# One tile mode at a time: padding PV's last keys, tails as entries of their own, and a new order for the first stretch

## The chip, the cores and the metric

The kernel runs on one core of a Trainium2 chip. The metric is device time in microseconds of one execution. The core's engines are TensorE (PE, with its weight loads PEld), VectorE (DVE), ScalarE (ACT), GpSimd (POOL) and SyncE (SP, which here only issues transfers). Each works through its own instructions in a fixed order and waits on semaphores for the others.

## The reference

Three layers follow each other. First attention with a memory: for 2 batches and 8 heads, 576 positions of 64 numbers,

```python
scores = scale * np.matmul(q, k.transpose(0, 1, 3, 2))
scores = np.where(causal, -1000000000.0, scores)
scores = scores - scores.max(-1, keepdims=True)
a = np.exp(scores)
a /= a.sum(-1, keepdims=True) + 1e-09
local = np.matmul(a, v)
mem_ret = np.einsum('bhsd,bhde->bhse', q_p, M_prev)     # q_p = phi(q)
mem_norm = np.einsum('bhsd,bhd->bhs', q_p, z_prev)[..., None] + 1e-06
return g * (mem_ret / mem_norm) + (1 - g) * local
```

Then, on the 1152 rows of 512 numbers that come out, `(x @ w1) * (x @ w2) @ w3 @ w_out` with weights given as 64-bit floats, and at last four experts, `p[:, e] * (relu(x @ w1[e]) @ w2[e])` summed over e. All of it is in 32-bit floats.

## The kernel before

**Stages.** The first stretch holds attention for all eight pairs of heads, the product W = w3 @ w_out (parts `w`), and the products of batch 0 with w1 and w2 (parts `b`). Then come W's product with batch 0 (`k`, tile `c`), the same for batch 1 (tiles `Zb`, `Rb`, `Qb`), and the four experts (tiles `Z`, `Q`, `R`, `o`).

**A pair of heads.** 576 positions are four blocks of 128 and one of 64. The two heads of a pair lie on partitions 0 to 63 and 64 to 127 of the query and key tiles. For pair p the parts are: `sp0` to `sp3`, scores of query blocks (0, 1), 2, 3 and of the last 64 queries of both heads (`scores`, tile `sc`); `mp*`, a masked reduction on VectorE that also copies the scores out of PSUM (`peaks`, tiles `P` and `mn`); `xp*`, the exponential on ScalarE; `tp0` to `tp6`, transposes of the probabilities in groups of up to four (`trans`, tile `pt`), and `cp*`, their copies to SBUF on ScalarE (tile `pT`); `vp0`, `vp1`, `vp2`, probabilities times V for head 0, head 1 and the last block of both (`pv`, `pv_last`, tile `a`); `np`, the memory product (`mem`, tile `b`); `jp`, `gp`, the divisions on VectorE (`join`, `mem_out`); `jap`, their sum on POOL; `zp`, the transposes of the result (`fin`, tile `x`), with `zhp` and `zlp` copying and splitting it.

**Shapes on TensorE.** Scores of the first four blocks contract over 64 partitions, so a head uses half of the array's rows. `pv` makes 64 output rows at a time: half of its columns. The last two matmuls of `pv_last` (j == NB) contract over 64 keys and make 64 rows: a quarter. The group `t6` transposes 64 columns. `mem` and `fin` end with a tail of two matmuls onto half of the columns. Everything else uses the whole array. 32-bit matmuls leave two records each in the trace, transposes and the bit-split products (`fp32r`) one.

**Weights.** 64-bit weights are rebuilt as floats: two ScalarE operations (`wa`, `oa`, `ba`: lines 129 and 130), two on VectorE (`wd`, `od`, `bd`: lines 136 and 137), then a split in a high and a low part, on POOL for w3, w1, w2 (`wp`, `bp`) and on ScalarE and VectorE for w_out (`oh`, `ol`). One tile of w3 feeds four groups of three matmuls (`wu_0` to `wu_3`), one of w1 or w2 two groups of twelve.

**What sets the order.** The string FIRST, written out by a planner, lists every part and every load (`@...`) of the first stretch; the program records the parts in this order, and each engine keeps it as its own queue. Nothing is reordered later. Tiles come from pools: `psS` has two PSUM buffers for scores, PV, memory and result tiles, `psT` two for transposes, so a part also waits for the reader of what its buffer held before.

Of the kernel before, what the change touches and what calls it, by code (L numbers as in the profile page):

```python
# [20 lines left out]
@o1 s11 c00 wp0 c02 t01 m10 @o2 x03 t04 c01 s12 @w1 c04 m11 x10 t03 m12 v00 @mz c03 x11 t05 @bt v01 c05 x12 t06 t10
s13 c06 c10 e2 v02 m13 @q3 oa0 t14 gates j0 @k3 t13 c14 n0 @V2 x13 od0 t11 t12 s20 g0 c11 @o3 c12 oa1 m20 v10 ja0 c13
x20 t16 v11 f2 oh0 od1 t15 e3 s21 c15 ol0 @w2 c16 oa2 v12 m21 w0_0 oh1 j1 @V3 x21 s22 od2 s23 m22 t20 wa1 @w3 t22 m23
c20 n1 @k4 x22 wd1 @q4 s30 c22 g1 wp1 @w4 x23 t24 oh2 t21 m30 z0 c24 c21 ja1 t23 zh0 v20 c23 zl0 x30 f3 v21 oa3 ol1
t25 ol2 t26 s31 c25 od3 c26 w0_1 hq4 hk4 v22 m31 lq4 @w5 wa2 w0_2 j2 s32 @V4 lk4 x31 n2 oh3 m32 e4 t30 wd2 x32 z1 t32
g2 c30 @w6 wa3 t31 ol3 s33 zh1 zl1 m33 wd3 c31 w0_3 @k5 c32 t34 ja2 y0 @w7 t33 c34 w1_0 c33 v30 @o4 f4 wa4 wp2 v31 x33
@b0 t35 @q5 z2 wd4 c35 @k6 t36 w1_1 zh2 @q6 wa5 w1_2 zl2 w1_3 c36 wd5 e5 n3 y1 wp3 v32 g3 w2_0 @V5 j3 w2_1 wa6 w2_2 f5
w2_3 w3_0 y2 wd6 w3_1 e6 w3_2 wp4 w3_3 s40 y3 wp5 s41 wa7 m40 w4_0 m41 w4_1 x40 ja3 w4_2 w4_3 x41 wd7 w5_0 y4 z3 wp6
oa4 w5_1 w5_2 zh3 w5_3 od4 w6_0 y5 w6_1 zl3 wp7 oh4 @o5 w6_2 ba0 w6_3 s42 ol4 y6 bd0 w7_0 w7_1 m42 oa5 bp0 @b1 w7_2
w7_3 x42 bs0 s43 od5 b0_0 y7 hk5 m43 @o6 oh5 lk5 b0_1 ba1 ol5 @k7 hq5 t40 bd1 x43 t41 n4 c40 lq5 c41 @b2 oa6 t44 g4  # L30
t43 bs1 bp1 c44 s50 @q7 bc00 bc01 t42 m50 v40 c42 c43 od6 x50 b1_0 f6 @b3 oh6 b1_1 ba2 ol6 rm00 e7 bd2 t45 rh00 v41
c45 rl00 ba3 @b4 rm01 bp2 s51 t46 rh01 bs2 m51 c46 v42 rl01 x51 bd3 b2_0 @V6 j4 ba4 bp3 @b5 b2_1 bc20 bs3 s52 bd4 bc21
b3_0 m52 ja4 ba5 @o7 b3_1 x52 bs4 rm10 bp4 rh10 s53 rm11 bd5 rl10 rh11 b4_0 hk6 hq6 rl11 oa7 @b6 b4_1 m53 bp5 x53 bs5
t54 bc40 t50 od7 bc41 c54 b5_0 c50 lq6 oh7 @b7 ba6 b5_1 rm20 bd6 ol7 rh20 t52 t51 c52 n5 rl20 c51 @w8 rm21 bp6 ba7 t53
g5 bs6 v50 rh21 c53 lk6 b6_0 rl21 bd7 b6_1 bc60 f7 wa8 @w9 t55 bp7 v51 bc61 bs7 c55 t56 s60 c56 wd8 b7_0 m60 wa9 wp8
@w10 v52 rm30 x60 b7_1 j5 @V7 rh30 wd9 w8_0 w8_1 rl30 wa10 @w11 w8_2 rm31 wp9 w8_3 rh31 s61 s62 wd10 w9_0 rl31 wa11
@w12 w9_1 m62 wp10 w9_2 y8 w9_3 x62 m61 ja5 s63 yh8 w10_0 m63 x61 w10_1 wd11 hq7 w10_2 hk7 w10_3 yl8 @w13 wa12 t64
wp11 y9 t62 z4 c64 yh9 t60 c62 wd12 n6 c60 x63 yl9 w11_0 @w14 wa13 g6 wp12 w11_1 w11_2 zh4 y10 w11_3 zl4 lq7 yh10
w12_0 w12_1 wd13 w12_2 w12_3 yl10 wa14 @w15 t61 t63 wp13 y11 z5 c61 yh11 v60 c63 wd14 zh5 w13_0 yl11 w13_1 wa15 @b8
zl5 wp14 w13_2 y12 w13_3 yh12 t65 v61 wd15 c65 w14_0 yl12 ba8 @b9 w14_1 wp15 y13 w14_2 yh13 w14_3 yl13 w15_0 bd8 w15_1  # L40
w15_2 y14 lk7 ba9 @b10 w15_3 t66 yh14 bp8 bs8 s70 c66 v62 m70 b8_0 yl14 y15 x70 bd9 s71 ba10 bp9 @b11 m71 b8_1 yh15
bs9 j6 x71 s72 yl15 t70 bd10 bc80 s73 bc81 c70 b9_0 m72 ja6 ba11 @b12 m73 x72 bs10 bp10 b9_1 rm40 rh40 x73 t71 rl40
b10_0 rm41 c71 bd11 rh41 b10_1 rl41 ba12 @b13 bp11 bc100 t74 bs11 bc101 t73 c74 z6 bd12 b11_0 zh6 bp12 @b14 ba13 zl6
b11_1 rm50 bs12 rh50 bd13 t72 b12_0 rl50 c72 @b15 rm51 bp13 c73 rh51 ba14 v70 bs13 rl51 bd14 t75 bc120 v71 c75 ba15
bs14 t76 n7 c76 bd15 b12_1 g7 bs15 v72 bc121 bp14 b13_0 j7 ja7 b13_1 rm60 rh60 rl60 z7 rm61 bp15 rh61 b14_0 zh7 zl7
b14_1 rl61 bc140 b15_0 bc141 b15_1 rm70 rh70 rl70 k00_0 rm71 rh71 k00_1 rl71 k00_2 k00_3 k01_0 kc00 k01_1 k01_2 k01_3
k10_0 kc01 k10_1 k10_2 k10_3 k11_0 kc10 k11_1 k11_2 k11_3 k20_0 kc11 k20_1 k20_2 k20_3 k21_0 kc20 k21_1 k21_2 k21_3
k30_0 kc21 k30_1 k30_2 k30_3 k31_0 kc30 k31_1 k31_2 k31_3 kc31
# [1115 lines left out]
```

## Time and profile before

| what | value |
|---|---|
| three runs | 686.61, 687.25, 687.84 us; median 687.25 |
| the profiled execution: span on the page | 685.4 us |
| its own time outside the span | not given; the median of the runs is 1.85 us above the span |
| busy TensorE, VectorE, ScalarE, POOL | 675.7, 447.5, 382.5, 368.6 us |
| first stretch (attention, w, b) | until 206.78 us, where the product `c` starts |

The page names for each group of instructions its source line, engine, operation and tiles. Times in the timeline are microseconds from the first instruction. A matmul's duration runs past the start of the next one, since they are pipelined: what a matmul costs is the distance from its start to the next start.

### The profile page before, as it was taken

The numbers are of one execution on the slowest core, as the hardware profiler recorded it, in microseconds if no ns is written. First come the engines' busy times: TensorE is split into PE (matmuls) and PEld (weight loads), VectorE is DVE, ScalarE is ACT, GpSimd is POOL, SyncE is SP. The second block draws the span as 40 slices with busy tenths as digits, with TensorE's granted clock in tenths as the row PEclk, the third lists the DMA queues.
The fourth block names the chain that finished last, engine by engine and source line by source line (L and its number), as shares of the span: only waits on it lengthen the run. The fifth ranks groups of instructions, "written<-read, shape, count | busy, mean of one in ns | idle before, by whom it ended". The sixth has DMA issues, their size and how long they took to land.

```text
span 685.4 us, 12814 instructions
## 1 busy us (share of the span) xinstructions
PE 675.7 (99%) x4877; PEld 605.1 (88%) x4877; DVE 447.5 (65%) x839; ACT 382.5 (56%) x808; POOL 368.6 (54%) x366
## 2 busy tenths in 40 slices
...
GB/s 286 176 169 219 71 198 192 174 109 124 185 139 34 90 62 94 55 35 98 62 62 123 77 109 62 112 73 107 79 121 64 62 124 64 122 61 109 154 32 62
DMA packets 43405, 74.53 MB, mean 109 GB/s; under 512 B 14416, under 2 KB 14416, under 8 KB 43344
## 3 DMA queue, kind: packets, MB, share of 16 engines
...
## 4 chain that ended last, share of the span: by engine, by line
PE 88%; DVE 6%; ACT 3%; issue 1%; DMA 1%; SPq 0%; DVEq 0%; ACTq 0%
PE o L990 28%; PE Z L1037 14%; PE c L587 7%; PE Q L1037 7%; PE wacc L473 7%; PE ab L537 5%; PE Zb L853 4%; PE R L1037 3%; PE a L330 2%; PE pt L307 2%; PE Qb L853 2%; PE sc L253 2%; ACT P L274 1%; DVE P L269 1%; PE Rb L853 1%
## 5 line engine op out<-in xcount | busy, mean ns | idle before, releaser
L990 PE MATMUL o<-w,he 128*128 128x512 f32 x864 | 224.8, 393 | 0.0
L104 POOL TENSOR_TENSOR w<-r,w 128x512 fp32r<-128x512 f32 x96 | 130.6, 1361 | 120.3 <-ACT w L728 120.2
L990 PEld LDWEIGHTS o<-w,he 128*128 128x128 f32 x864 | 153.8, 188 | 24.1
L975 ACT ACTIVATE he<-t 128x320 fp32r<-128x320 f32 (+1 forms) x96 | 42.7, 445 | 120.6 <-DVE t L1066 73.3
L976 DVE SCALAR_TENSOR_TENSOR he<-t,he 128x320 fp32r<-128x320 f32 (+1 forms) x96 | 57.4, 598 | 49.1 <-ACT he L975 49.1
L1059 DVE TENSOR_TENSOR t<-u,Q 128x320 f32<-128x320 f32 (+1 forms) x32 | 14.6, 455 | 83.2 <-ACT u L1057 83.2
L107 DVE TENSOR_TENSOR w<-r,w 128x512 fp32r<-128x512 f32 x64 | 66.2, 1036 | 0.0
L728 ACT CAST w<-r 128x512 fp32r<-128x512 f32 x96 | 58.9, 614 | 0.0
L537 PE MATMUL ab<-xT,ws 128*128 128x288 f32 x384 | 55.4, 299 | 1.2 <-ACT asb L547 0.7
L537 PEld LDWEIGHTS ab<-xT,ws 128*128 128x128 f32 x384 | 51.5, 188 | 3.1 <-issue 1.3
L587 PE MATMUL c<-hT,W 128*128 128x288 f32 (+2 forms) x384 | 52.6, 295 | 0.0
L587 PEld LDWEIGHTS c<-hT,W 128*128 128x128 f32 x384 | 51.6, 188 | 0.0
L1037 PE MATMUL Z<-X0T,w 128*128 128x320 f32 x288 | 50.2, 310 | 0.2 <-ACT s L1047 0.2
L1037 PEld LDWEIGHTS Z<-X0T,w 128*128 128x128 f32 x288 | 46.0, 188 | 4.4 <-ACT s L1047 0.6
L473 PE MATMUL wacc<-wo,w3s 128*128 128x512 f32 x192 | 48.2, 400 | 0.0
L1037 PEld LDWEIGHTS Z<-X1T,w 128*128 128x128 f32 x288 | 40.8, 189 | 4.1
L473 PEld LDWEIGHTS wacc<-wo,w3s 128*128 128x128 f32 x192 | 35.0, 188 | 8.8 <-issue 1.0
L1037 PE MATMUL Z<-X1T,w 128*128 128x256 f32 x288 | 42.1, 282 | 0.0
L269 DVE CUSTOM_DVE_ANT_0 P<-sc,mask 128x128 f32<-128x128 f32 (+4 forms) x72 | 33.7, 516 | 11.4 <-PE sc L253 6.4
L758 ACT CAST w<-r 128x512 fp32r<-128x512 f32 x64 | 39.5, 619 | 0.0
L274 ACT ACTIVATE P<-P,mn 128x128 f32<-128x128 f32 (+4 forms) x72 | 37.7, 582 | 1.0 <-DVE mn L269 0.9
L101 POOL TENSOR_SCALAR w3s<-tf_l 128x512 fp32r<-128x512 f32 x16 | 12.8, 799 | 43.9 <-DVE tf_l L137 33.3
...
## 6 DMA issues: line engine op xcount, KB each, us to landing
...
```

The lines of the kernel that those rows point to most:

```text
L104: nc.gpsimd.tensor_sub(dst, src, r32(hi))
L107: nc.vector.tensor_sub(dst, src, r32(hi))
L274: nc.scalar.activation(Pt[i, x], Pt[i, x], AF.Exp, bias=one, scale=-1.0)
L473: nc.tensor.matmul(wacc[u], lhsT=w3s[u][:, a, c, :], rhs=wo[4 * g + c][:, bb, :], start=(c == 0 and x == 0), stop=(c == 3 and x == 2),)
L537: nc.tensor.matmul(ps[:, 0:HS], lhsT=self.ws[u][:, wi, kk, :], rhs=xT[b, kk][:, xi, a * HS : (a + 1) * HS], start=(n == 0), stop=(n == 3 * ...
L587: nc.tensor.matmul(st["ps"], lhsT=Wt[kk][:, wi, d * P : (d + 1) * P], rhs=hT[kk][:, xi, t0 : t0 + tw], start=(kk == 0 and x == 0), stop=(k ...
L728: return lambda: nc.scalar.copy(st["w"][i][:, 0], src(i))
L853: nc.tensor.matmul(st[d], lhsT=b1_set[m][a][:, wi, kk, :], rhs=BX[b][:, xi, kk, :], start=first and kk == 0 and x == 0, stop=(kk == 1 and ...
L975: nc.scalar.activation(h[:, 0], src, AF.Relu)
L976: nc.vector.scalar_tensor_tensor(out=h[:, 1], in0=src, scalar=0.0, in1=r32(h[:, 0]), op0=ALU.max, op1=ALU.subtract)
L990: nc.tensor.matmul(o_ps[i], lhsT=h_of[s][x][:, a, i * P : (i + 1) * P], rhs=w2s[s][x][:, b, :], start=first, stop=last,)
L1037: nc.tensor.matmul(ps, lhsT=w1s[s][a][:, wi, kk, :], rhs=X[c, b][:, xi, kk, :], start=first and kk == 0 and x == 0, stop=(kk == 1 and x == ...
```

## The change

`t6` now transposes 128 columns (the last 64 keys and 64 others that are there anyway), and the last step of `pv_last` contracts over all 128 rows. The 64 extra rows of V are zero already; a memset puts a zero into the added column of ones too, so that the extra rows add nothing. The tails of `mem` and `fin` become parts of their own, `nt` and `zt`. FIRST is planned anew, with matmuls of one mode of the array together.

```diff
-@q0 @k0 @k1 @q1 e0 @V0 f0 s00 s01 @w0 m00 e1 m01 s02 x00 @V1 f1 s03 @o0 x01 m02 wa0 t00 @k2 t02 m03 @q2 s10 x02 wd0
+@q0 @k0 @w0 @k1 @q1 @o0 @mz e0 @bt s00 f0 @w1 s01 @o3 m00 wa0 m01 s02 x00 s10 m02 x01 t02 wd0 x02 s03 t03 c02 wp0 @k3
...
     for t in v4:
         nc.gpsimd.memset(t[:, :, D : D + 1], 1.0)
+        nc.gpsimd.memset(t[SB:P, NB, D : D + 1], 0.0)
...
-            kr = SB if mine[0][2] == NB else P
...
-                st[g] = ps = psT.tile([P, 512], F32, tag="T", name=f"pt{g}_{p}")[0:kr, 0 : P * len(mine)]
+                st[g] = ps = psT.tile([P, 512], F32, tag="T", name=f"pt{g}_{p}")[:, 0 : P * len(mine)]
...
-                    nc.tensor.transpose(ps[:, y * P : (y + 1) * P], prob_t[p][i, x][:, k0 : k0 + kr], identF)
+                    nc.tensor.transpose(ps[:, y * P : (y + 1) * P], prob_t[p][i, x][:, k0 : k0 + P], identF)
...
-                t = A1.tile([kr, P * len(mine)], F32, tag=f"pt{g}", name=f"pT{g}_{p}")
+                t = A1.tile([P, P * len(mine)], F32, tag=f"pt{g}", name=f"pT{g}_{p}")
...
-                kr = SB if j == NB else P
                 for x, o in enumerate(halves):
                     nc.tensor.matmul(
-                        st["a"][0][o, NB], lhsT=pt[NB, 0, j][:, o], rhs=v4[(2 * p + x) % 4][0:kr, j, :],
+                        st["a"][0][o, NB], lhsT=pt[NB, 0, j][:, o], rhs=v4[(2 * p + x) % 4][:, j, :],
...
+
+        def mem_last():
             for x in range(2):
                 nc.tensor.matmul(
-                    m[0][x * SB : (x + 1) * SB, NB], lhsT=phi_t[p][:, NB * P : S], rhs=mz[:, p, x], start=True, stop=True
+                    st["n"][0][x * SB : (x + 1) * SB, NB], lhsT=phi_t[p][:, NB * P : S], rhs=mz[:, p, x], start=True, stop=True
                 )
...
-            for x in range(2):
-                o = slice(x * SB, (x + 1) * SB)
-                nc.tensor.matmul(ps[o, NB * P :], lhsT=st["q"][:, NB], rhs=identF[:, o], start=True, stop=True)
+
+        def fin_last():
+            for x, o in enumerate(halves):
+                nc.tensor.matmul(st["x"][o, NB * P :], lhsT=st["q"][:, NB], rhs=identF[:, o], start=True, stop=True)
```

TensorE before, where pair 0's PV begins (`a0`; `pt5_0` is group 5 of pair 0's transposes, `sc4_1` the scores of pair 1's last queries, 64x65 an output on half of the columns):

```order
L330 MATMUL a0_296<-v0_104,pT0_0_241 64x65 x8
L330 MATMUL a0_296<-v0_104,pT1_0_270 64x65 x8
L330 MATMUL a0_296<-v0_104,pT4_0_277 64x65 x4
L307 MATMUL pt5_0_322<-identF_84,P4_0_223 128x128 x4
L330 MATMUL a0_296<-v1_105,pT2_0_246 64x65 x8
L330 MATMUL a0_296<-v1_105,pT3_0_318 64x65 x8
L330 MATMUL a0_296<-v1_105,pT4_0_277 64x65 x4
L307 MATMUL pt6_0_352<-identF_84,P4_0_223 64x128
L307 MATMUL pt0_1_354<-identF_84,P0_2_254 128x128
L307 MATMUL pt0_1_354<-identF_84,P1_2_258 128x128 x2
L307 MATMUL pt0_1_354<-identF_84,P2_2_279 128x128
L242 MATMUL sc4_1_359<-kd1_148,qd1_150 128x288 x2
```

TensorE now, at the same place:

```order
L307 MATMUL pt6_0_319<-identF_84,P4_0_238 128x128
L363 MATMUL b0_321<-mz_103,phi0_169 128x130 x4
L369 MATMUL b0_321<-mz_103,phi0_169 64x65 x2
L330 MATMUL a0_336<-v0_104,pT0_0_300 64x65 x8
L330 MATMUL a0_336<-v0_104,pT1_0_331 64x65 x8
L330 MATMUL a0_336<-v0_104,pT4_0_263 64x65 x4
L330 MATMUL a0_336<-v1_105,pT2_0_231 64x65 x8
L330 MATMUL a0_336<-v1_105,pT3_0_277 64x65 x8
L330 MATMUL a0_336<-v1_105,pT4_0_263 64x65 x4
L339 MATMUL a0_336<-v0_104,pT5_0_304 64x65
L339 MATMUL a0_336<-v1_105,pT5_0_304 64x65
```

Before, transposes and scores stood between head 0, head 1 and the last block of PV; now all transposes of pair 0 come first, the tail of `b0` stands against PV, and nothing stands between the two heads.

VectorE before, from pair 1's `phi` on (`P3_0` and `P4_0` are the 512- and 576-wide reductions of pair 0, `P0_2` the first of pair 1, `tf_l30` the first w3 tile's conversion; the short rows read out a minimum):

```order
L221 TENSOR_SCALAR ex1_178<-ex1_178 128x576
L222 SCALAR_TENSOR_TENSOR phi1_193<-qd1_150,ex1_178 128x576
L269 ISA P3_0_203,mn0_169<-sc3_0_184,mask_85 128x512
L269 ISA mn0_169 128x1
L269 ISA P3_1_205,mn0_169<-sc3_0_184,mask_85 128x512
L269 ISA mn0_169 128x1
L269 ISA P4_0_223,mn0_169<-sc4_0_196,mask_85 128x576
L269 ISA mn0_169 128x1
L136 SCALAR_TENSOR_TENSOR tf_l30_207<-tf_l30_207,tu_l30_208 128x512
L137 SCALAR_TENSOR_TENSOR tf_l30_207<-w3r0_167,tf_l30_207 128x512
L269 ISA P0_2_254,mn1_253<-sc0_1_227,mask_85 128x128
L269 ISA mn1_253 128x1
```

VectorE now, at the same place in its queue:

```order
L270 ISA P3_0_208,mn0_179<-sc3_0_196,mask_85 128x512
L270 ISA mn0_179 128x1
L270 ISA P3_1_210,mn0_179<-sc3_0_196,mask_85 128x512
L270 ISA mn0_179 128x1
L136 SCALAR_TENSOR_TENSOR tf_l30_188<-tf_l30_188,tu_l30_189 128x512
L137 SCALAR_TENSOR_TENSOR tf_l30_188<-w3r0_152,tf_l30_188 128x512
L270 ISA P4_0_238,mn0_179<-sc4_0_223,mask_85 128x576
L270 ISA mn0_179 128x1
L270 ISA P0_2_252,mn1_251<-sc0_1_203,mask_85 128x128
L270 ISA mn1_251 128x1
L270 ISA P0_3_254,mn1_251<-sc0_1_203,mask_85 128x128
L270 ISA mn1_251 128x1
```

Pair 1's `phi` has gone further back, and the conversion of the first w3 tile, which stood behind pair 0's 576-wide reduction, now stands ahead of it.

## Rows read from the trace of the kernel before

**Rows 1.** The page, part 1: busy us (share of the span) and instructions of TensorE.

```profile
PE 675.7 (99%) x4877; PEld 605.1 (88%) x4877; DVE 447.5 (65%) x839; ACT 382.5 (56%) x808; POOL 368.6 (54%) x366
```

**Rows 2.** Busy us by stretch: PE, PEld, DVE, ACT, POOL, clock, DMA, GB/s.

```profile
0.00:20.00 20.00, 17.05 (x159) 12.11 (x160) 11.07 (x40) 14.50 (x29) 4.09 (x16) 1.00 0.92 291
...
sum 207.50, PE 201.83 PEld 169.44 DVE 168.40 ACT 150.12 POOL 96.44; mean PE 18.35 PEld 15.40 DVE 15.31 ACT 13.65 POOL 8.77
```

**Rows 3.** TensorE's waits, 0 to 265 us: us in total, times, longest.

```profile
PE warm L188 <- POOL v L174: 2.0, 1, 2.0
PE pt L307 <- ACT pT L311: 1.1, 2, 0.7
```

**Rows 4.** Timeline of TensorE, 16 to 25 us: start, us, line, names, shapes, count.

```profile
16.14 1.39 PE L330 MATMUL a<-v,pT 128*64 128x65 f32 x40
17.46 0.66 PE L307 MATMUL pt<-identF,P 128*128 128x128 f32 x4
18.04 1.39 PE L330 MATMUL a<-v,pT 128*64 128x65 f32 x40
...
21.88 1.09 PE L307 MATMUL pt<-identF,P 128*128 128x128 f32 x8
22.80 1.06 PE L364 MATMUL b<-mz,phi 128*128 128x130 f32 x8
23.79 0.34 PE L368 MATMUL b<-mz,phi 128*64 128x65 f32 x4
24.06 0.66 PE L307 MATMUL pt<-identF,P 128*128 128x128 f32 x4
```

**Rows 5.** Timeline of TensorE, 41 to 44 us, pair 2's PV.

```profile
41.19 2.55 PE L330 MATMUL a<-v,pT 128*64 128x65 f32 x80
43.67 0.77 PE L307 MATMUL pt<-identF,P 128*128 128x128 f32 x5
```

**Rows 6.** Timeline of VectorE, 6 to 14 us.

```profile
6.77 0.29 DVE L269 CUSTOM_DVE_ANT_0 P<-sc,mask 128x128 f32<-128x128 f32 x1 [1.04 <-PE sc L253]
...
7.89 0.55 DVE L269 CUSTOM_DVE_ANT_0 P<-sc,mask 128x384 f32<-128x384 f32 x1
...
8.85 0.46 DVE L221 TENSOR_SCALAR ex<-ex 128x576 f32<-128x576 f32 x1
...
10.01 0.68 DVE L269 CUSTOM_DVE_ANT_0 P<-sc,mask 128x512 f32<-128x512 f32 x1
...
11.23 0.76 DVE L269 CUSTOM_DVE_ANT_0 P<-sc,mask 128x576 f32<-128x576 f32 x1
...
11.91 0.69 DVE L136 SCALAR_TENSOR_TENSOR tf_l<-tf_l,tu_l 128x512 uint32<-128x512 uint32 x1
...
13.24 0.28 DVE L269 CUSTOM_DVE_ANT_0 P<-sc,mask 128x128 f32<-128x128 f32 x1
```

**Rows 7.** Timeline of ScalarE, 7 to 14 us.

```profile
7.46 0.68 ACT L216 ACTIVATE ex<-qd 128x576 f32<-128x576 f32 x1 [3.02 <-DMA qd<-in_q_cols_dram]
...
10.45 0.69 ACT L129 ACTIVATE tu_l<-w3r 128x512 uint32<-128x512 uint16 x1
...
11.58 1.33 ACT L274 ACTIVATE P<-P,mn 128x512 f32<-128x512 f32 x2
12.80 1.05 ACT L311 COPY pT<-pt 128x512 f32<-128x512 f32 x2
13.74 0.79 ACT L274 ACTIVATE P<-P,mn 128x576 f32<-128x576 f32 x1
```

**Rows 8.** Timeline of all engines, the end of the first stretch.

```profile
200.31 6.63 PE L537 MATMUL ab<-xT,ws 128*128 128x288 f32 x48
...
200.48 21.79 SPq L792 DMA_DIRECT2D wr<-wf  x8
...
206.78 22.40 PE L587 MATMUL c<-hT,W 128*128 128x288 f32 x168
...
229.02 0.96 PE L853 MATMUL Zb<-BXB,b1w 128*128 128x288 f32 x6
```

More of the change, by code (lines that the diff above doesn't have):

```diff
@@ L19 @@
 FIRST = """
-@q0 @k0 @k1 @q1 e0 @V0 f0 s00 s01 @w0 m00 e1 m01 s02 x00 @V1 f1 s03 @o0 x01 m02 wa0 t00 @k2 t02 m03 @q2 s10 x02 wd0
[L21 to L48, printed above, removed]
+@q0 @k0 @w0 @k1 @q1 @o0 @mz e0 @bt s00 f0 @w1 s01 @o3 m00 wa0 m01 s02 x00 s10 m02 x01 t02 wd0 x02 s03 t03 c02 wp0 @k3
@@ new lines @@
+m03 oa0 t04 @V0 m10 s12 c04 x03 @o1 s11 m12 @q2 c03 @V1 x12 t00 m11 t05 s13 c00 od0 c05 t01 gates @k2 e1 t06 n0 @o2
+m13 oh0 c01 ol0 nt0 v00 c06 oa1 g0 v01 x13 od1 x10 v02 s20 j0 x11 t10 oh1 m20 t11 ja0 oa2 s22 ol1 s21 c11 od2 c10 w0_0
+m21 t14 x21 f1 t13 s23 c13 m22 oh2 @q3 t16 w0_1 @V2 c16 c14 t15 m23 wa1 n1 t12 c15 wd1 nt1 c12 v10 oa3 g1 @w2 wp1 v11
+e2 x22 f2 v12 w1_0 @V3 x20 od3 t24 t23 w1_1 c24 j1 @w3 c23 z0 @q4 oh3 @w4 zt0 ol2 wa2 @w5 s30 ol3 @k4 ja1 x23 w0_2 wd2
+zh0 w0_3 wa3 t22 zl0 @o6 w1_2 wp2 m30 c22 y0 s32 s31 m32 x32 w1_3 wd3 t21 y1 w2_0 hq4 m31 @b4 t25 wp3 c21 @w7 w2_1 wa4
@@ new lines @@
+@w6 t20 w2_2 lq4 c20 wd4 w2_3 c25 t26 z1 c26 wp4 x31 zt1 v20 y2 v21 wa5 zh1 v22 wd5 w3_0 wa6 w3_1 zl1 x30 w3_2 j2 s33
+wd6 w3_3 wa7 t32 m33 @o4 w4_0 wp5 wd7 x33 n2 hk4 w4_1 c32 t34 y3 lk4 @b0 w4_2 c34 t36 oa4 w4_3 t33 y4 wp7 od4 nt2 c36
+s40 c33 w5_0 g2 ba0 @o5 w5_1 e3 t30 m40 x40 w5_2 bd0 w5_3 t31 oh4 y5 f3 wp6 s42 c31 s41 c30 m42 @q5 e4 w7_0 @k5 oa5
+t35 @V4 m41 ja2 w6_0 n3 ol4 @k6 f4 @b1 nt3 v30 g3 e5 c35 v31 od5 v32 @b3 w7_1 ba1 j3 s43 oh5 w6_1 ja3 hk5 m43 n4 hq5
+f5 lk5 x41 z2 bd1 nt4 zt2 x42 w7_2 lq5 w7_3 ol5 @b2 zh2 t44 bs1 y7 zl2 w6_2 bp0 bs0 oa6 @q6 g4 t42 w6_3 z3 od6 y6 bp1
@@ new lines @@
+zt3 s50 zh3 oh6 zl3 b0_0 ba2 ol6 e6 bd2 b0_1 c44 ba3 m50 @b5 s53 bs2 bc00 bp2 bc01 t43 m53 s52 bd3 x53 s51 ba4 b1_0
+bs3 @o7 c42 bd4 x43 b1_1 rm00 bs4 rh00 ba5 t46 b2_0 rm01 bp3 rl00 rh01 c46 m51 c43 t45 b2_1 rl01 bd5 bc20 t41 m52 b3_0
+@b7 bp4 c41 bs5 bc21 x52 t40 rm10 b3_1 oa7 c40 od7 n5 c45 bp5 v40 @b6 oh7 hk6 ol7 nt5 v41 rh10 x51 rl10 rm11 lk6 v42
+hq6 x50 b4_1 j4 ba6 f6 ja4 t51 t56 b4_0 c56 g5 rh11 lq6 t50 rl11 s61 bd6 s60 bc40 bc41 ba7 b5_0 m60 @w8 bp6 c50 @k7
+c51 m61 s63 t52 m63 z4 b5_1 rm20 bd7 rh20 rl20 s62 @w9 bp7 rm21 @q7 rh21 b6_0 @V6 x61 rl21 wa8 @V5 b6_1 bc60 wd8 t54
```

17 lines of the change are left out of this document (15 added, 2 removed).

## Prediction

> **What bounds the kernel now.** I read the page's first part, then the busy time by stretch, then TensorE's waits, and last its timeline, instruction by instruction, where matmuls of different shapes meet. The reader is to see that TensorE is the bound everywhere: busy 675.7 of 685.4 us [rows 1]. The change touches only the first stretch, which ends where the output product `c` begins at 206.78 [rows 8]; there TensorE is busy 201.83 of 207.5 us [rows 2], and besides the 2.0 us before its first matmul its largest wait is 1.1 us in sum [rows 3]. Its granted clock is 1.00 in every stretch, so its higher level, and nothing is taken for the clock. What shortens this kernel must therefore shorten TensorE's own work in the first stretch.
>
> Busy time hides something here. A matmul uses the whole array (128*128), half of its rows (64*128: scores of the first four query blocks), half of its columns (128*64: PV and the tails) or a quarter (64*64: the last 64 keys of PV). I call each a mode. In [rows 4] the 40 records of one head's PV start at 16.14 and the next group at 17.46: 1.32 us. In [rows 5] two heads' PV stand together, 80 records in 2.48 us, so 1.16 more for the second 40. A head that stands alone pays 0.16 more when it is left. The four transposes between the two heads take 0.58 (17.46 to 18.04), where eight that follow each other take 0.92 (21.88 to 22.80), so 0.46 for four: another 0.12. There and back costs 0.28. The tails agree: eight records of `b` take 0.99 until the tail starts (22.80 to 23.79), and the tail's four records 0.27, where four of 80 records in one mode take 0.12. **One change of mode costs about 0.145 us**, during which TensorE counts as busy.
>
> Where modes don't change but a group does (21.88 to 22.80, transposes to `b`) there is no such surplus: eight take 0.115 each. So it is the mode, not the new group.
>
> The Trainium skill says the same in words (TensorEngine Tiling (Array Packing), Key Properties): changing the tiling mode drains TensorE. Its page TensorE: Matmul & The Clock Gate (Step-by-step: what each phase is for) puts a drain at some 128 cycles, by my estimate 0.053 us at 2.4 GHz; by that the 60 changes below would be worth 3.2 us and the forecast 685.5. The rows' 0.145 is nearly three times as much, and the rows decide.
>
> **The change, part by part.**
>
> *Fewer changes of mode.* Counting along TensorE's whole order, mode by mode, I find 111 changes before and 51 after, all in the first stretch. The padded tail takes away the eight 64*64 entries of `pv_last` and the eight 64-column transposes; the split-off tails of `b` and `x` go where a neighbour has 128*64 already; and each pair's PV now stands as one block of 100 records (first two fences of the section on the change). 60 x 0.145 = 8.7 us less. Bounds: 60 x 0.12 = 7.2 and 60 x 0.16 = 9.6.
>
> *Padding.* The transpose `t6` streams the same 128 columns of the identity, and the two last matmuls of `pv_last` the same 65 columns; only rows are added. No row shows a padded tail; the nearest are the first eight matmuls of the same group, which use all 128 rows and whose records stand 0.031 apart like any of PV [rows 5], so I take 0, with 0.1 us either way. The copy of `t6` keeps 128 elements a partition. A rule of the skill speaks against padding (TensorEngine Tiling (Array Packing), When to Use Tiling): a contraction of 64 should be row-tiled, two at once. By it the padded tails would lose at most their own time again, 16 matmuls, an estimate of 0.5 us; no row here shows two of these running at once over row halves.
>
> *Four small memsets on POOL*, of one element on 64 partitions each, stand behind the identity that the first transposes wait for, before POOL's first split. POOL has nothing due there. 0.
>
> *The new order.* This is what may eat the gain. TensorE does the same 4373 matmuls, but the others must have their inputs ready in a new order. In before, the start of any group is 2.0 us (the first matmul) + the work before it + 0.145 for each change + what was lost in waits. The work is the sum of distances between starts where the mode stays (0.115 a transpose or less, 0.031 a record of PV, 0.135 a record of `ab`: 48 between 200.31 and 206.78 [rows 8]), 179.4 us for the stretch. So 206.78 - 2.0 - 179.4 - 111 x 0.145 = 9.3 us were lost by the end; in the same way 2.4 by 20 us and 4.5 by 47. What is it now? I follow the new order by hand for the first 44 us, where VectorE and ScalarE set the pace, with distances between starts in [rows 6, 7].
>
> VectorE starts at 6.77, as before, and now holds (last two fences) 1.12 for pair 0's first four reductions, 0.96 for the next two, then 1.22 for the 512-wide ones, which must await their scores (9.1 + 0.3), so 10.6; then the conversion of the first w3 tile, 1.33, now ahead of the 576-wide reduction, 0.68; then pair 1's first four, 1.12: 13.75. Behind the conversion stands the bank that pair 1's 512-wide scores need, so these begin at 13.9 and not sooner: TensorE idles about 0.8 us. Their reductions end at 16.4, and the last scores of pair 1 begin at 16.55. ScalarE then has two exponentials of 512 (1.22 the pair), copies of 0.47, the gates and some single operations of 0.57 before the copy that the second half of PV needs, at 19.8; VectorE's bank for PV is free at 19.6. PV of pair 0 starts at 19.7 with 13.3 us of work and 5 changes behind it: loss 19.7 - 2 - 13.3 - 0.7 = 3.7, against 2.4 in before at equal work. With the busy durations in place of the distances it comes 1.4 later.
>
> From there ScalarE has hardly a gap: exponentials, transposed copies, and a conversion of 1.13 per weight tile. Pair 1's first transposes wait for its exponentials until 24.3; pair 3's 512-wide scores wait for VectorE's split of `xT` until 42.2. The fourth group of w3 tile 1 starts at 44.0 with 35.3 us of work and 16 changes behind it: loss 4.4, about before's 4.5 there. With the longer durations it starts at 47.3: loss 7.7. So the new order costs between 0 and 3.2 us more waiting. I take 1.3, nearer the distances between starts, since these are what the rows of a dense queue show. Behind 44 us the products of w3 and w1/w2 (2.7 and 3.2 us of TensorE for each tile, one conversion of 1.13 on ScalarE) give the other engines room again, and I cost the rest as before.
>
> *Loads.* The first w3 tile moves to third in SP's queue, ahead of pair 1's keys and queries. Pair 1's queries had landed at 7.46 in before, when the exponential that waited for them began [rows 7]; 512 KB more at the 291 GB/s of the first 20 us [rows 2] make it 9.3. Pair 1's first scores are due at 9.1: 0.2 at most, inside the 1.3. V moves back behind two weight tiles and is due only at 19.7.
>
> *The end of the stretch.* Pairs 6 and 7 are now finished after the last product `ab`, so the first reads back of `wf`, issued at 200.48 in before, 6.3 us ahead of `c`, are issued when `c` begins. They feed the first `Zb`, which starts 22.2 us after `c` [rows 8]. VectorE's work between is late by some 1.1 us and has that cover. 0; if it were gone, 1.1.
>
> *Sum*: -8.7 + 1.3 = -7.4. The profiled execution's span, 685.4, becomes 678.0; the median of the runs shown, 687.25, lies 1.85 above that span, so 679.9, say **680.0 us**.
>
> **Rivals.**
>
> *Only part of the surplus goes.* The 0.145 has two parts: about 0.095 until the next group starts, and 0.05 because its first matmul takes longer. If the second belongs to any group that starts behind a wait, only 60 x 0.095 = 5.7 goes: -5.7 + 1.3, so 682.9. For it: new groups stand behind copies. Against: the transposes to `b` above. In its favour as a drain rule speaks the skill's page named above.
>
> *The queue that feeds takes all.* ScalarE and VectorE are dense until 60 us; if each of the six later pairs loses 0.8 on top of the longer walk, as pair 1's 512-wide scores do above, 3.2 + 6 x 0.8 = 8 goes: 686.6, no change. Against: VectorE idles for 39 us and ScalarE for 57 of the 207.5 [rows 2].
>
> *Slower.* ScalarE's queue is fixed. If in each of the eight pairs one weight conversion, 1.13, stands ahead of a copy that TensorE needs and nothing covers it, that is 9.0, with the longer walk's 3.2 12.2 against 8.7: +3.5, so 690.8. It decides from five uncovered conversions on (3.2 + 5.7). For it: the conversions of w3 0 and of two w_out tiles now stand ahead of pair 1's exponentials. Against: w3 products stand ready on TensorE from 27 us on.
>
> *All of it comes, and waits shrink too*: -9.6, so 677.6.
>
> **How the numbers follow.** Forecast 0.60 (own range 678.3 to 682); partial 0.12; all 0.10; no change 0.10; slower 0.08. The range 677.5 to 685.0 leaves out the last two. What a measurement of this kernel can tell from no change is 0.2%, 1.4 us: faster takes the forecast, the partial and the full case and a little of the queue's, 0.84; same 0.09; slower 0.07.
>
> **What would show it.** The first `c` starts at about 199.4 and not 206.78, and everything behind it keeps its length. TensorE's busy time falls by about 8 us, its idle time grows by 1 to 2. A pair's PV stands as 100 records in about 3.0 us. PV of pair 0 starts at 19.7 to 21.1. It would be wrong if the loss in waits at 44 us were over 8 us, if TensorE's idle time grew by more than 4, if `Zb` waited, or if single tails within their mode still cost 0.27.

## The result, and the profile after

| | before | after |
|---|---|---|
| runs (median) | 686.61 to 687.84 (687.26) | 693.45 to 697.07 (695.86) |
| ratio of the medians, 95% interval | | 1.012 (1.010 to 1.014) |
| span of the profiled execution | 685.4 | 694.4 |
| first `c` | 206.78 | 215.46 |

The change makes the kernel slower by 8.6 us; the forecast was 680.0. Nearly the whole difference lies in the first stretch. These are the rows of the changed kernel's timeline that answer to [rows 8] (start, us, engine, line, names, shapes, count):

```profile
215.46 22.51 PE L589 MATMUL c<-hT,W 128*128 128x288 f32 x168
...
215.63 17.70 SPq L794 DMA_DIRECT2D wr<-wf  x8
...
237.81 0.96 PE L855 MATMUL Zb<-BXB,b1w 128*128 128x288 f32 x6
```

`c` starts 8.7 us later, and the reads of `wf` are issued with it, as forecast. `Zb` still follows `c` by 22.35 us (22.24 before), so hardly anything behind the stretch has changed.

TensorE's line of the page's first part, and then busy us by stretch (columns as in [rows 2]):

```profile
PE 672.0 (97%) x4877; PEld 604.1 (87%) x4877; DVE 453.4 (65%) x839; ACT 381.8 (55%) x808; POOL 372.5 (54%) x370
```

```profile
0.00:20.00 20.00, 15.52 (x82) 10.78 (x82) 11.41 (x41) 13.00 (x25) 4.26 (x20) 0.91 0.78 266
...
60.00:80.00 20.00, 17.28 (x180) 14.18 (x180) 18.77 (x40) 14.15 (x28) 10.30 (x8) 1.00 0.42 129
80.00:100.00 20.00, 17.29 (x140) 14.53 (x134) 16.24 (x37) 13.41 (x25) 9.75 (x9) 0.91 0.48 145
...
sum 215.40, PE 197.09 PEld 167.55 DVE 171.98 ACT 147.60 POOL 96.50; mean PE 17.92 PEld 15.23 DVE 15.63 ACT 13.42 POOL 8.77
```

TensorE has 3.7 us less of busy time and is still 97% busy. Behind the first 20 us it idles most between 60 and 100 us, where VectorE is full (18.77 of 20 us) and then ScalarE thin (13.41 of 20). Its granted clock, 1.00 everywhere before, is 0.91 in two stretches. Its waits (us in total, times, longest) tell more:

```profile
PE pt L307 <- ACT P L275: 3.1, 3, 2.4
PE warm L189 <- POOL v L174: 2.0, 1, 2.0
PE wacc L475 <- ACT half L486: 1.6, 1, 1.6
PE wacc L475 <- DVE both L489: 1.5, 2, 1.1
PE ab L539 <- ACT asb L549: 1.5, 1, 1.5
PE pt L307 <- ACT pT L311: 1.4, 3, 0.9
PE sc L254 <- DMA qd<-in_q_cols_dram: 1.2, 1, 1.2
PE wacc L475 <- POOL w3s L104: 1.2, 1, 1.2
PE b L363 <- DVE mn L270: 1.2, 1, 1.2
PE ab L539 <- DVE ra L349: 1.1, 1, 1.1
```

Before, the largest besides the first matmul's was 1.1 us in sum [rows 3]. Now nine reach that, for ScalarE, VectorE, GpSimd (POOL in the rows) and a load. No single one explains 8.6 us.

The forecast's sum can be run backwards: the start of `c` is 2.0 us, 179.4 us of work, 0.145 for each change of mode, and the loss in waits. Before that was 9.3 of loss with 111 changes. Now 215.46 - 2.0 - 179.4 - 51 x 0.145 leaves 26.7. So 8.7 us were saved and 17.4 more were lost. Of these 17.4 the windows show 12.6 as idle time of TensorE (215.40 - 197.09 = 18.3 us now, 207.50 - 201.83 = 5.7 before [rows 2]). The other 4.8 stand inside its busy time, where the lower clock counts too: at most 0.09 of two stretches of 20 us, so 3.6 us. The saving itself can be seen in TensorE's timeline (start, us, line, shapes, count):

```profile
52.29 0.60 PE L392 MATMUL x<-identF,xq 128*128 128x128 f32 x4
52.82 0.34 PE L398 MATMUL x<-identF,xq 128*64 128x64 f32 x4
52.99 2.50 PE L330 MATMUL a<-v,pT 128*64 128x65 f32 x80
55.32 0.75 PE L339 MATMUL a<-v,pT 128*64 128x65 f32 x20
56.00 2.32 PE L475 MATMUL wacc<-wo,w3s 128*128 128x512 f32 x9
```

Pair 2's PV takes 3.01 us as one block (52.99 to 56.00), as forecast, and the tail of `x` in front of it 0.17 us, where a tail of `b` took 0.27 [rows 4].

### The profile page after: what moved, and what is told of

It reads as the page before. It is cut to its first block, busy times and chain, and to the rows that moved or that the text cites. A ratio compares the mean times of both kernels' runs of the same rounds, so it can differ in the third digit from the quotient of the medians.

```text
span 694.4 us, 12811 instructions
## 1 busy us (share of the span) xinstructions
PE 672.0 (97%) x4877; PEld 604.1 (87%) x4877; DVE 453.4 (65%) x839; ACT 381.8 (55%) x808; POOL 372.5 (54%) x370
## 4 chain that ended last, share of the span: by engine, by line
PE 57%; DVE 2%; ACT 1%; issue 0%
PE o L992 28%; PE Z L1039 14%; PE Q L1039 7%; PE c L589 4%; PE R L1039 3%; PE Zb L855 1%; PE Qb L855 1%; DVE w L107 0%; DVE x L676 0%; DVE he L978 0%; ACT he L977 0%; DVE X1B L107 0%; DVE prs L783 0%; ACT w L730 0%; DVE t L1068 0%
## 5 line engine op out<-in xcount | busy, mean ns | idle before, releaser
L475 PE MATMUL wacc<-wo,w3s 128*128 128x512 f32 x192 | 55.7, 420 | 4.8 <-ACT half L486 1.6
L475 PEld LDWEIGHTS wacc<-wo,w3s 128*128 128x128 f32 x192 | 34.0, 193 | 14.2 <-issue 3.6
L307 PE MATMUL pt<-identF,P 128*128 128x128 f32 x200 | 32.2, 285 | 4.4 <-ACT P L275 3.1
```

The lines of the kernel that those rows point to most:

```text
L475: nc.tensor.matmul(wacc[u], lhsT=w3s[u][:, a, c, :], rhs=wo[4 * g + c][:, bb, :], start=(c == 0 and x == 0), stop=(c == 3 and x == 2),)
```

## The experiments

All are edits of the changed kernel's code or order; "padded" means its code in the order of before. The time is the median, the ratio that to runs of the kernel before on the same chip, with its 95% interval. "Loss" is the sum above run backwards.

### Is it the padding, or putting modes together?

**Padding alone.** Each tail stands directly behind its group, all else as before.

```diff
-... n0 @V2 ... z0 c24 ...
+... n0 nt0 @V2 ... z0 zt0 c24 ...
```

> The kernel before with the padded tail alone (its own order, each tail directly behind its group): 105 changes of mode instead of 111. Theory (the new order makes TensorE wait for late producers, 17.4 us more lost in waits, and the mode price of 0.145 us is real): -6 x 0.145 = -0.9 us, so 686.4 (685.5 to 687.3); its first c starts 0.9 earlier. Rival A (the padding or the split of the tails costs time itself): slower than 688, at 689 to 696 if it were the whole of the 8.6 us. Rival B (the price of a mode change is a wait in disguise): 687.3, no change.

Measured: 686.71 us, 0.9987 (0.9977 to 0.9996); `c` at 205.84, 0.94 earlier. That is what six changes of mode at 0.145 give if padding costs nothing. The trace shows the two parts. Here is pair 0's last PV block, before and now, each with the start that follows:

```profile
21.00 0.95 PE L340 MATMUL a<-v,pT 128*64 128x65 f32 x20
21.88 1.09 PE L307 MATMUL pt<-identF,P 128*128 128x128 f32 x8
...
21.13 0.80 PE L339 MATMUL a<-v,pT 128*64 128x65 f32 x20
21.86 1.09 PE L307 MATMUL pt<-identF,P 128*128 128x128 f32 x8
```

It takes 0.73 us to the next start and took 0.88. Over the eight pairs these blocks take 5.82 us, 7.15 before. The eight padded transposes take 1.59 us to the next start, 1.41 before. So padding costs about 0.02 us a pair, and the price falls away with the change of mode. Not every change that the count adds has the price: pair 1's padded transpose between two PV parts, now two changes more, takes 0.257 us in place of 0.229.

**Each pair's PV in one block**, only this moved (TensorE's entries of pair 0):

```diff
-t03 v00 t05 v01 t06 t10 s13 v02
+t03 t05 t06 t10 s13 v00 v01 v02
```

> The padded kernel in the order of before, with one thing moved on TensorE alone: each pair's PV stands as one block of 100 records, where its last part stood. 81 changes of mode. Theory: 30 fewer changes than before, -4.35 us, less up to 2 us of new waiting because two thirds of each PV come some 1 to 3 us later: 684.0 (682.9 to 685.5). Rival B (no price for a mode change, the surplus moves to a wait): 686.5 to 688. Rival A (padding costs): as in the padded kernel plus the same saving, above 688.

Measured: 696.54 us, 1.0134 (1.0119 to 1.0149). That is a miss for the theory and for rival B: 30 fewer changes than before and 9 us slower. Rival A's "above 688" takes it in, but the padded kernel has ruled rival A out. TensorE's timeline of this kernel shows how; in brackets is the idle time before and what ended it:

```profile
16.09 1.09 PE L307 MATMUL pt<-identF,P 128*128 128x128 f32 x8
17.93 0.33 PE L307 MATMUL pt<-identF,P 128*128 128x128 f32 x1 [0.75 <-ACT pT L311]
19.42 0.66 PE L307 MATMUL pt<-identF,P 128*128 128x128 f32 x4 [1.16 <-ACT pT L311]
...
20.98 2.56 PE L330 MATMUL a<-v,pT 128*64 128x65 f32 x80
```

In the old order the two parts of PV at 16.14 and 18.04 ran between these transposes [rows 4], while ScalarE copied the group before. There are two banks for transposes; with PV gone from between them, the third group waits for a copy. At 20.98 the loss is 5.3, against 2.5 in the padded kernel; it is 22.6 at the end, against 9.2. Up to `c` TensorE waits 5.0 us in sum for such copies, against 1.7. The old order's changes of mode were the price of cover.

**As many changes saved, cover kept.** 14 groups move by at most some 2 us to a neighbour of their mode (a tail that now comes first also opens its bank), for example:

```diff
-t03 v00 t05 v01 t06 ... v02 t14 t13 n0 nt0 ... n2 nt2 t30 z1 zt1
+t03 t05 v00 v01 t06 ... v02 nt0 t14 t13 n0 ... n2 z1 nt2 zt1 t30
```

> The padded kernel in the order of before, with 14 groups on TensorE moved by at most about 2 us to a neighbour of their mode (tails of b and x, four groups of transposes or PV parts, pair 4's PV together), the other parts of each PV left between the transposes, as before. 81 changes of mode, as many as in the kernel with each pair's PV in one block, which took 696.5. Theory (the price of a change is real, and what a plan loses is the work that covered ScalarE's copies): -24 x 0.145 = -3.5 us against the padded kernel's 686.7, so 683.2 (682.5 to 685). Rival H (fewer changes always bring as many waits, whichever groups are moved): 686 to 697.

Measured: 686.94 us, 0.9990 (0.9981 to 1.0000). Again 81 changes, now no slower, but not faster either: rival H. From t03 to t06 it takes 3.51 us in place of 3.80, so two changes do give 0.29. But TensorE comes to the next hand-over before its input. In the padded kernel the products of w3 tiles 2 and 3 run on without a stop (first row), in this one TensorE waits for GpSimd in the middle (the other two):

```profile
64.33 5.06 PE L475 MATMUL wacc<-wo,w3s 128*128 128x512 f32 x21
```

```profile
64.10 3.02 PE L487 MATMUL wacc<-wo,w3s 128*128 128x512 f32 x12
67.94 1.40 PE L487 MATMUL wacc<-wo,w3s 128*128 128x512 f32 x5 [0.82 <-POOL w3s L101]
```

Tile 3's first matmul then starts at 67.94 and not at 67.19. The loss is 13.1 against 9.2. Taken from start to start, less the work, 19 places with a wait in front of them lose 10.9 us here and 10 such places 6.7 in the padded kernel, while a change of mode with no wait in front costs 0.13 us in both. So the changes saved are real, and what they gave came back at late inputs.

### Does one bad place make the new order slow?

**A load first, and keys first.** Left the b1 load, right the first w3 tile's.

```diff
-... m42 @q5 e4 w7_0 @k5 oa5 t35 @V4 ... @k6 f4 @b1 nt3 ...
+... m42 @b1 @q5 e4 w7_0 @k5 oa5 t35 @V4 ... @k6 f4 nt3 ...
```
```diff
-@q0 @k0 @w0 @k1 @q1 @o0 ...
+@q0 @k0 @k1 @q1 @w0 @o0 ...
```

> The changed kernel with one entry moved on SyncE's queue: the load of the weight tile b1 goes ahead of the load of pair 5's queries, which waits for the third phi. Theory: the load is issued when its staging buffer comes free, at 72.9 and not at 78.6, and lands by 77 to 78; ScalarE's 4.28 us wait for it at 84.7 goes, and with it most of the 4.6 us that TensorE lost between 86 and 94 us (its 2.4 us wait for a softmax included): -2 to -4.5 us, so 691.4 to 694, the clock of 80:100 back above 0.95. Rival C (the clock's fall is the cause, the load not): within 1 us of the changed kernel's 695.9. Rival D (VectorE and ScalarE are full there anyway, what is won is lost until 110 us): 695 to 696, the loss at 107 us still 17.

> The changed kernel with the first w3 tile's load behind pair 1's keys and queries, as before, not ahead of them. Theory: pair 1's queries land at 7.4 and not at 9.4, the wait of 1.22 us at 9.5 goes; VectorE's reductions pace TensorE there, so that 0.5 to 1.2 us are won, 694.7 to 695.4; the w3 tile lands some 2 us later and is not waited for before 13 us. The granted clock of the first 20 us rises from 0.91 if it was the wait that lowered it. Rival C (the clock is lower because of the new order of work, whatever the waits): clock still 0.91 in 0:20, 695.5 to 696.

Measured: 696.45 us, 1.0130 (1.0113 to 1.0147), and 696.35 us, 1.0131 (1.0116 to 1.0146). Neither gains; both are a little slower than their theories and rivals had it. The changed kernel's rows at that place are (ScalarE three times, then TensorE):

```profile
75.30 0.68 ACT L217 ACTIVATE ex<-qd 128x576 f32<-128x576 f32 x1 [1.17 <-DVE phi L223]
...
79.25 0.68 ACT L217 ACTIVATE ex<-qd 128x576 f32<-128x576 f32 x1 [2.14 <-DVE phi L223]
...
84.68 0.68 ACT L129 ACTIVATE tu<-wr 128x512 uint32<-128x512 uint16 x1 [4.28 <-DMA wr<-in_moe_w_tiles_dram]
...
89.32 0.44 PE L307 MATMUL pt<-identF,P 128*128 128x128 f32 x2 [2.38 <-ACT P L275]
```

With the load first ScalarE's 4.28 us and TensorE's 2.38 us are gone, but TensorE then waits 3.05 us for VectorE at 93.0. With the keys first pair 1's scores start at 8.34 and not at 9.54, but the conversion of the w3 tile, which stands early in ScalarE's and VectorE's queues, now waits for its load, and pair 0's PV starts at 22.09 and not at 20.90.

**Load first and two buffers for phi's exponential**, so that ScalarE doesn't wait for VectorE's phi (first two rows above).

```diff
-st["ex"] = ex = A1.tile([P, S], F32, tag="ex", ...)
+st["ex"] = ex = A2.tile([P, S], F32, tag="ex", ...)
```

> The changed kernel with the b1 load ahead of pair 5's queries (as in the run that moved only that load, 696.4) and with two buffers instead of one for phi's exponential, so that ScalarE no longer waits for VectorE's phi (1.2 and 2.1 us at 75 to 79). Theory K (ScalarE's and SyncE's fixed queues stood behind one late entry): 3 to 5 us less, 691 to 693. Rival L (VectorE is late there in its own right, its operations slowed beside GpSimd's): 695 to 697.

Measured: 695.86 us, 1.0122 (1.0105 to 1.0139). Theory K falls; the time is in rival L's range.

**TensorE kept busy**, for the clock.

```diff
+            if p == 1 and qb[0] == 0:
+                for _ in range(8):
+                    nc.tensor.transpose(ps[:, 0, 0:P], identF, identF)
...
+                for _ in range({(0, 3): 4, (4, 4): 16}.get((p, g), 0)):
+                    nc.tensor.transpose(ps[:, 0:P], identF, identF)
```

> The changed kernel with spare transposes of the identity ahead of three groups that TensorE waited for (8 ahead of pair 1's first scores, 4 ahead of t03, 16 ahead of t44), into banks that the group then overwrites. They fill waits of 1.2, 0.5 and 2.4 us. Theory (the clock falls because TensorE waits, and costs little where others set the pace): the granted clock of 0:20 and 80:100 rises from 0.91, the time stays within 694.5 to 697. Rival C (the fallen clock is what costs): 3 us and more come back, 690 to 693.

Measured: 694.28 us, 1.0097 (1.0081 to 1.0113). The clock is 1.00 in every stretch, and `c` starts at 213.16. Over the four executions the mean granted clock is 0.998 to 1.000, against 0.993 to 0.997 in the changed kernel's four, so filling the waits does raise it. By the medians that is worth 1.6 us of the 8.6, a little more than the theory's range allows and less than rival C's 3, but the two intervals overlap. No single dip can be put down to a single wait: in the trace without the low parts of w_out (below) TensorE is idle for 3.7 of the 12 us from 84 to 96, and the clock stays at 1.00.

**The new order up to pair 3's PV, then the old.** The first part ends with `v32`; what is left follows in the order of before.

> The changed kernel's order up to pair 3's PV block, then everything that is left in the order of before (tails padded). 81 changes of mode. Theory (waits come wherever work of one mode is put together, in both halves): the new order's loss of 12.6 us by that block stays, the later half loses about 4 as in before and not 14: c starts at 2.0 + 179.4 + 81 x 0.145 + 16.5 = 209.6, so 690 (688 to 692). Rival F (one bad place in the first half, around 70 to 95 us, makes all of it): 693 to 696. Rival G (only the later half is bad): 683 to 686.

Measured: 695.68 us (692.45 to 699.67), 1.0120 (1.0080 to 1.0161): a miss for the theory. The number lies in rival F's range, but the trace doesn't show rival F's one place alone. Where the two orders meet, between 80 and 94 us, the loss grows by 7.5 to 18.7 (by 4.8 in the new order alone); the granted clock is 0.72 there from 84 to 96. Behind that the old order adds 3.9, where the new order adds 10.0 (16.7 to 26.7). Waits come in both halves, but the total is not settled by this run.

### Which engine sets the pace?

**A third of the w3 products left out**, in the padded kernel and in the changed one (part of the product is missing):

```diff
-        for x, (a, bb) in enumerate(PASSES):
+        for x, (a, bb) in enumerate(PASSES[1:]):
...
-                start=(c == 0 and x == 0), stop=(c == 3 and x == 2),
+                start=(c == 0 and x == 0), stop=(c == 3 and x == 1),
```

> The padded kernel in the order of before (686.7) with a third of the w3 products' matmuls left out (64 of 512 columns, 0.225 us each: 14.4 us of TensorE between 32 and 165 us; a part of the product is missing). New theory (TensorE, though busy 97%, already runs in the first stretch at the pace of VectorE, ScalarE and GpSimd; what it saves comes back as waits): 3 to 8 us less, 679 to 684, and its waits grow by 6 to 11. Rival I (TensorE is the bound there, as the prediction had it): 12 to 14.4 less, 672.3 to 675.

> The changed kernel with the same third of the w3 products' matmuls left out (14.4 us of TensorE). Theory (the changed kernel's first stretch runs at the pace of the other engines even more than that of before, where 3.5 of the 14.4 showed): 0 to 4 less, 692 to 696. Rival I (TensorE is the bound): 681.5 to 684.

Measured: 683.18 us, 0.9937 (0.9913 to 0.9962), and 693.07 us, 1.0081 (1.0066 to 1.0096). So 14.4 us of TensorE's work are worth 3.5 us in the old order and 2.8 in the new, as the two theories had it. The 3.5 is a middle: two executions at a mean granted clock of 1.000 took 681.2 and 682.3 us, two at 0.997 took 684.0 and 684.6. The rest comes back as waits, in the old order for ScalarE's copies and GpSimd's splits:

```profile
PE wacc L475 <- ACT half L486: 2.7, 1, 2.7
PE pt L307 <- ACT pT L311: 2.6, 3, 1.0
PE wacc L475 <- POOL w3s L104: 2.2, 4, 1.5
...
PE ab L539 <- POOL ws L104: 1.0, 1, 1.0
```

So in the old order the pace of the other engines lies only some 2 to 5.5 us below TensorE's, though TensorE is busy 99% of the span [rows 1]. And with TensorE relieved the new order is still 9.9 us slower than the old: it is the engines that feed TensorE that take longer.

**VectorE relieved.** The low parts of w_out are left out in the changed kernel, in the padded one, in the padded one without the third of w3, and in the order with 81 changes and cover; in one more they move to GpSimd, with nothing left out.

```diff
-            f"ol{c}": lambda: lo_dve(wo[c][:, 1, :], st["f"], wo[c][:, 0, :]),
+            f"ol{c}": lambda: None,
...
-                wacc[u], lhsT=w3s[u][:, a, c, :], rhs=wo[4 * g + c][:, bb, :],
+                wacc[u], lhsT=w3s[u][:, a, c, :], rhs=wo[4 * g + c][:, 0, :],
```

> The changed kernel without the low parts of w_out: VectorE's eight subtractions for them (0.69 to 1.89 us each, 8.6 us in sum, seven of them before 95 us) are left out, and TensorE uses the high part in their place, with as many matmuls (so part of the product is left out). Theory, as far as VectorE sets the pace where TensorE waits (70 to 95 us): 3 to 6 us less, 690 to 693. Rival D (ScalarE's fixed queue and the loads set it): less than 1.5 us, 694.5 to 696.

> The padded kernel in the order of before without VectorE's eight subtractions for the low parts of w_out (7.2 us of VectorE, none of TensorE; a part of the product is missing). New theory: its 7 us of waits shrink a little, 1 to 3 less, 683.7 to 685.7. Rival I (TensorE is the bound): no change, 686.2 to 687.

> The padded kernel in the order of before with both left out: a third of the w3 products' matmuls (14.4 us of TensorE; alone 683.2) and VectorE's eight subtractions for the low parts of w_out (7.2 us; alone 686.9). A part of the product is missing. If VectorE is what the shortened TensorE waits for: 1.5 to 4 below 683.2, 679 to 681.7. Rival M (no one engine: the turns between ScalarE, VectorE, GpSimd and their few buffers set the pace): 682.2 to 684.

> The same leaving-out of VectorE's eight subtractions in the order with 81 changes of mode and the tails near (686.9). New theory: here the saved changes show as soon as VectorE is relieved, 1.5 to 3.5 below the padded kernel with the same leaving-out, so 681 to 684. Rival I with no price for a change: as the padded kernel with the same leaving-out.

> The order with 81 changes of mode, the eight subtractions moved from VectorE to GpSimd (nothing left out). VectorE has 7.2 us less, GpSimd 8 times about 1.4, so 11 us more of its own work. New theory, if VectorE is the engine that sets the pace: 1 to 3 less than 686.9, 684 to 686. Rival J (GpSimd's work slows VectorE by as much, or GpSimd sets the pace): 687 to 690.

Measured: 693.40 us, 1.0087 (1.0072 to 1.0102); 686.87, 0.9987 (0.9977 to 0.9996); 683.61, 0.9942 (0.9928 to 0.9957); 686.02, 0.9979 (0.9970 to 0.9989); 687.06, 0.9996 (0.9986 to 1.0005). In the old order VectorE alone holds nothing up, with or without TensorE's third (rivals I and M). In the new order some 2.5 us hang on it, between the theory's 3 and rival D's 1.5. In the order with 81 changes 0.9 us do, less than the theory's 1.5, and the intervals with and without overlap; with the work moved to GpSimd nothing is won (rival J).

**Two exponential buffers in the order with 81 changes and cover**, nothing left out (edit as above).

> The order with 81 changes of mode and the tails near (686.9), with two buffers instead of one for phi's exponential, nothing left out. If a blocked ScalarE queue hides the saved changes there too: 1 to 3 less, 684 to 686. Rival M: 686 to 687.5.

Measured: 686.57 us, 0.9982 (0.9973 to 0.9992). Rival M. With padding alone this is the best version that computes everything: 0.9 to 1.1 us faster than before, 0.1 to 0.2%.

**GpSimd relieved**, in both orders:

```diff
-            lo_pool(w3s[u][:, 1], st["f"], w3s[u][:, 0])
...
-                wacc[u], lhsT=w3s[u][:, a, c, :], rhs=wo[4 * g + c][:, bb, :],
+                wacc[u], lhsT=w3s[u][:, 0, c, :], rhs=wo[4 * g + c][:, bb, :],
```

(and the same for the `b` tiles)

> The changed kernel without GpSimd's low parts of the 32 weight tiles of the first stretch (about 1.35 us each, 43 us of GpSimd; TensorE uses the high part in their place with as many matmuls, so a part of the product is missing). Rival L (VectorE's operations, slowed beside GpSimd's, make the new order late): 4 to 8 us less, 688 to 692, and far more of its gain than the old order shows in the run beside it. Theory N (late hand-overs between ScalarE, VectorE and the loads, whatever GpSimd does): at most 2.5 less, 693.4 to 696.

> The same left out of the padded kernel in the order of before (686.7). It shows what relief of GpSimd and VectorE is worth where TensorE hardly waits: 0 to 2 less, 684.7 to 686.9.

Measured: 685.97 us, 0.9989 (0.9968 to 1.0009; single executions 684.5 to 691.2), and 686.73 us, 0.9990 (0.9981 to 1.0000). Rival L, and more than it asked for: the same 43 us of GpSimd are worth 9.9 us in the new order and nothing in the old. The new order's loss falls from 26.7 to 15.1, by 4.1 us between 68 and 97 and by 5.4 between 147 and 190 (times of the changed kernel, at equal work). That trace is of the fastest execution, with a granted clock of 1.00 throughout, so up to 3.6 us of these 11.6 can be the clock's. And even without the splits the new order is hardly faster than the old (0.8 us, inside the intervals), with 54 fewer changes of mode. Here is the place at 70 us in the changed kernel, GpSimd and VectorE in turn:

```profile
70.68 1.65 POOL L104 TENSOR_TENSOR w3s<-tf_l,w3s 128x512 fp32r<-128x512 f32 x1
...
71.23 1.65 DVE L137 SCALAR_TENSOR_TENSOR tf<-wr,tf 128x512 uint32<-128x512 uint32 x1
...
72.29 1.86 POOL L382 TENSOR_TENSOR xq<-xq,xm 128x576 f32<-128x576 f32 x1
...
72.80 1.67 DVE L222 TENSOR_SCALAR ex<-ex 128x576 f32<-128x576 f32 x1
...
74.51 0.76 DVE L223 SCALAR_TENSOR_TENSOR phi<-qd,ex 128x576 f32<-128x576 f32 x1
```

The operation at L137 starts while GpSimd's split of a w3 tile runs and ends 0.55 us behind it: 1.65 us. The operation with one input at 72.80 is held up too, 1.67 us beside GpSimd's sum of a pair (L382), where it took 0.46 in [rows 6]. The same operation without the split lasts 0.69 us (first row of the relieved kernel, where GpSimd's pair sum still slows the third):

```profile
68.32 0.69 DVE L137 SCALAR_TENSOR_TENSOR tf<-wr,tf 128x512 uint32<-128x512 uint32 x1
...
68.93 0.87 DVE L222 TENSOR_SCALAR ex<-ex 128x576 f32<-128x576 f32 x1
...
69.84 1.86 DVE L223 SCALAR_TENSOR_TENSOR phi<-qd,ex 128x576 f32<-128x576 f32 x1
```

The Trainium skill tells why such a pair takes turns (SBUF — State Buffer, SBUF: two separate sides): VectorE with two SBUF inputs and GpSimd share a pair of ports, which the one that starts first holds for its whole instruction. The two rows at 70.68 and 71.23 agree.

Behind L137 stand phi, pair 4's reductions and the copies that TensorE, ScalarE and SyncE's next load wait for. In the relieved kernel TensorE's largest waits are

```profile
PE warm L189 <- POOL v L174: 2.0, 1, 2.0
PE pt L307 <- ACT P L275: 1.7, 3, 1.0
PE pt L307 <- ACT pT L311: 1.1, 1, 1.1
PE sc L254 <- DVE ra L349: 0.9, 1, 0.9
```

The old order's VectorE is slowed as well. These are the means of one kind of operation (16 times, `tf_l` at L136) in before, in the changed kernel and in the relieved one:

```profile
L136 DVE SCALAR_TENSOR_TENSOR tf_l<-tf_l,tu_l 128x512 uint32<-128x512 uint32 x16 | 17.0, 1061 | 0.4 <-ACT tf_l L130 0.4
```

```profile
L136 DVE SCALAR_TENSOR_TENSOR tf_l<-tf_l,tu_l 128x512 uint32<-128x512 uint32 x16 | 15.4, 961 | 6.1 <-ACT tf_l L130 6.1
```

```profile
L136 DVE SCALAR_TENSOR_TENSOR tf_l<-tf_l,tu_l 128x512 uint32<-128x512 uint32 x16 | 11.0, 689 | 8.9 <-ACT tf_l L130 8.9
```

1.06 us before, 0.96 in the changed kernel, 0.69 without the splits. So the new order doesn't slow VectorE more. By the rows at 70 us it puts slowed operations in front of what TensorE needs next, where the old one has other work ready. That it is VectorE's lateness and not GpSimd's own is read from the waits: up to 204 us in the changed kernel TensorE waits 1.2 us for a result of GpSimd behind its first matmul, ScalarE 1.1 and VectorE nothing, while VectorE's busy time falls from 167.8 to 156.8 us without the splits. In the old order it falls by as much and more, from 168.2 to 150.7, and nothing is won.

## Why the prediction was wrong

- **The price of a change of mode** (60 x 0.145 = 8.7) held: the PV block, the tails, six changes for 0.94 us, two for 0.29, and, from start to start in seven traces, 0.13 to 0.15 us for a change with no wait in front.
- **Padding and memsets at 0** held: 686.71, with some 0.02 us a pair for the padded transpose.
- **The end of the stretch at 0** held: 22.35 us from `c` to `Zb`.
- **What bounds the kernel** failed. "What shortens this kernel must therefore shorten TensorE's own work" is necessary, not sufficient: 14.4 us of that work are worth 3.5. Few waits [rows 3] showed that TensorE was the last to be ready, not how far the others were behind. The forecast's own signs say so: TensorE's busy time fell by 3.7 us and not by 8, and its idle time up to `c` grew by 12.6, where more than 4 was to show it wrong.
- **The new order at +1.3** is the term that made the sum wrong: +17.4 was measured. Up to 47 us the walk was near: pair 0's PV at 20.90 (19.7 to 21.1 forecast), the last group of w3 tile 1 at 47.28 (44.0 to 47.3), a loss of 7.7 against 4.5, the 3.2 more of its upper end. Which durations were right can't be told from that: in two other traces with the same order up to there (load first; new, then old order), whose clock was 1.00 from 8 to 16 us, that PV starts at 19.8 and 19.7 and that group at 48.1 and 46.7. The load term in it was 0.2 and is 0.6 to 1.2 in these three: TensorE waited for pair 1's queries. "Behind 44 us ... I cost the rest as before" is the step that failed: 14.2 of the 17.4 are lost behind 47 us. There VectorE works beside GpSimd between 70 and 95 and between 147 and 185 us, and single operations take 1.65 us and more; the walk had them at 0.69, from a row at 11.91 [rows 6], before GpSimd's first split at 13.50.
- **The rival on the slower side** had ScalarE's queue as the cause and 690.8. The side was right, and ScalarE does wait: 30.5 us for VectorE and 20.4 for loads up to `c`, against 21.9 and 12.5 before (sums over its waits). But it waits for late inputs; the conversion at 84.68 held its queue for 4.28 us because the load was late, not by the 1.13 of its own work. Its chance of 0.08 (0.07 for slower) was too small, as was that of no change.
- **The clock** wasn't in the sum. Its fall to 0.91 in two stretches costs about 1.6 us by the medians, which the intervals can't tell from nothing, and 3.6 at most.

Open: no run takes VectorE's slowing away and leaves GpSimd's results as they are, so that part rests on the waits. Of the 17.4 us, 5.8 stay without the splits (15.1 of loss against 9.3), and their cause isn't known. Nor is it known which engine holds 11 of the 14.4 us in the old order. More buffers than the second one for `ex` weren't tried.
